# Attention keys in tiles of 128 with a shared slot for the rest, all scores inside FFN1 in groups of three, and centering in three steps

## The chip, the cores and the metric

The kernel runs on one core of one Trainium2 chip. The metric is the device time of one execution in microseconds (us), as the median of several executions.

The engines are called PE (TensorE, matmul), DVE (VectorE), ACT (ScalarE), POOL (GpSimd) and SP (SyncE, which here issues DMAs only).

## The reference, cut to what matters

```python
q, k, v: (8, 12, 448, 64)               # batch, heads, sequence, head size
scores = q @ k.T / sqrt(64)
attn   = max(scores, 0)**2 / 448        # no softmax: score tiles are independent
x      = attn @ v                       # -> (8, 448, 768)
xn     = (x - mean) / sqrt(var + 1e-6) * g_ln
out    = x + max(xn @ w_ch1, 0) @ w_ch2 # FFN, 768 -> 3072 -> 768
```

448 tokens are 3.5 tiles of 128.

## The kernel before: the parts that matter

Batch after batch, PE does FFN1 (24 groups of twelve matmuls), then FFN2. FFN2 works on pairs of 128-token tiles by a seven-product scheme of Strassen's kind. A batch has one or two such pairs (one in batches 0 and 4, where batch 0 uses the plain product); half tiles are carried over. The attention of batch b+1 is woven into batch b, in "excursions": a few score tiles between FFN matmuls. A "pair" of heads is two heads of 64 rows; a batch has six pairs.

```python
def att_T(i):                    # queries and keys of pair i, from batch 2 on: DMA transposes
    for t in range(2):
        nc.sync.dma_start_transpose(qkT[i][:, t, :]..., qk_ring[:, i % 3, t])
...
def att_QK(i, t, ...):           # one score slot: 112 keys x 448 queries, both heads
    for hh in range(2):
        nc.tensor.matmul(half[:SP, :S], qkT[i][r, 1, t*SP:(t+1)*SP], qkT[i][r, 0, :], ...)
...
def ffn_x(b, ki):                # the tokens of batch b back to token-major (x_tok has 5 slots)
    m0 = ts[0]
    while m0 < ts[-1] + 1:
        m1 = min(ts[-1] + 1, m0 + NT - m0 % NT)      # NT = 5: a batch that wraps needs two
        nc.sync.dma_start_transpose(x_tok[:, m0 % NT:...], xT[:, ki, ...])
        m0 = m1
...
def excursion(n, ...):
    while loads: load_qk(loads.pop(0))               # POOL issues loads
    if ready: att_AV(ready.pop(0), ...)              # weighted sum of values of a finished pair
    took = [slots.pop(0) for _ in range(n)]
    for m, (i, t) in enumerate(took): att_QK(i, t, ...)
    ...                                              # squares on DVE
    for i, t in took:
        if t == NJ - 1:
            ready.append(i); queued(i)               # queued(i): att_T(i + 3), later load_qk(i + 6)
...
def ffn_1_all(b):
    for ni in range(K2):                             # 24 groups
        if 3 <= ni < 3 + K1: ffn_x(b, ni - 3)        # x_tok transposes, six feature blocks
        ffn_1(ni)
        if m >= 0 and ni % 2 == 0: ffn_stats(ms[m])  # row statistics on DVE, late in FFN1
        if 0 < b < B - 1 and ni in IN_FFN1[b]: excursion(3, relus=(2,))
```

Both kinds of DMA transpose are issued by SP, in program order. Those of pair i+3 are put into the program when the last scores of pair i are; there are three qkT buffers.

## Time and profile before

| | before |
|---|---|
| time, median of 3 (lowest to highest); with a fourth execution 542.81 us | 542.84 us (541.98 to 544.71) |
| PE busy, granted clock | 97% of the span, 1.00 |
| FFN1 / FFN2 of a batch with two tile pairs (2, 3, 6) | 36.08 / 30.89 us |
| FFN1 / FFN2 of batch 4 (one pair) | 39.11 / 16.17 us |
| FFN1 of batch 7, which has no scores | 27.24 us |

A stage's length is the time from its first FFN matmul to the first one of the next stage, read from the timeline of matmuls. These are from the page of the kernel before: busy us of an engine with its share of the span, and the granted PE clock in 40 slices, in tenths.

```profile
PE 527.1 (97%) x5729; PEld 341.6 (63%) x5729; DVE 369.6 (68%) x660; ACT 306.6 (57%) x487; POOL 204.3 (38%) x261
...
PEclk9999999999999999999999999999999999999999
```

PE is the bottleneck, so what counts is which matmuls start late. The next lines are PE's timeline in FFN1 of batch 5: start and length in us, engine, source line, what is written from what, how many, and in brackets the idle time before and what ended it. L225 is the score matmul, L322 FFN1.

```profile
368.64 0.59 PE L225 MATMUL sc<-qkT_t 64*112 64x448 bf16 x4
...
369.35 3.60 PE L322 MATMUL f<-xc,w 128*64 128x448 bf16 x36
372.87 0.40 PE L225 MATMUL sc<-qkT_t 64*112 64x448 bf16 x2
374.14 0.40 PE L225 MATMUL sc<-qkT_t 64*112 64x448 bf16 x2 [0.87 <-DMA qkT_t<-qk_ring]
```

From the first line to the FFN1 line is an excursion without a wait: three slots in 0.71 us (368.64 to 369.35), against 3 x 0.189 us of streaming. The last line is a wait for a transpose of queries and keys. Its bracket gives PE's idle time, 0.87 us; from start to start it is 1.08 us (374.14 less 372.87, less the usual 0.19 us of one slot). Below, waits are told from start to start, so they are up to 0.2 us longer than the brackets. The SP queue in the same stretch shows why it came late (L300 issues x_tok transposes, L202 those of queries and keys):

```profile
350.41 7.61 SPq L300 DMA_TRANSPOSE x_tok<-xT  x6
358.19 2.50 SPq L202 DMA_TRANSPOSE qkT_t<-qk_ring  x2
360.73 8.63 SPq L300 DMA_TRANSPOSE x_tok<-xT  x6
369.53 6.51 SPq L202 DMA_TRANSPOSE qkT_t<-qk_ring  x5
```

Two transposes take 2.50 us, six take 7.61: about 1.25 us each, and SP does nothing else meanwhile. For 19 us it only works through transposes; batch 5 needs twelve for x_tok, because its four tiles wrap around the five slots.

The other thing that holds PE is centering in FFN2. This is DVE's timeline in FFN2 of batch 5 (L288 centers, L432 takes a product out of PSUM):

```profile
398.10 3.64 DVE L288 SCALAR_TENSOR_TENSOR xc<-f,g_sb,xc 128x448 bf16<-128x448 f32 x6 [2.67 <-PE f L282]
401.66 0.55 DVE L432 TENSOR_TENSOR acc<-f,acc 128x384 f32<-128x384 f32 x1
```

And this is PE's timeline behind it (L384 is a matmul of a product):

```profile
402.26 1.98 PE L384 MATMUL f<-w,h 128*64 128x384 bf16 x22 [0.36 <-DVE acc L432]
```

Six centering steps run in a row, and PE then waits for the evacuation behind them. From start to start the product is 0.53 us late.

### The profile page before, as it was taken

The numbers are of one execution on the slowest core, as the hardware profiler recorded it, in microseconds if no ns is written. First come the engines' busy times: TensorE is split into PE (matmuls) and PEld (weight loads), VectorE is DVE, ScalarE is ACT, GpSimd is POOL, SyncE is SP. The second block draws the span as 40 slices with busy tenths as digits, with TensorE's granted clock in tenths as the row PEclk, the third lists the DMA queues.
The fourth block names the chain that finished last, engine by engine and source line by source line (L and its number), as shares of the span: only waits on it lengthen the run. The fifth ranks groups of instructions, "written<-read, shape, count | busy, mean of one in ns | idle before, by whom it ended". The sixth has DMA issues, their size and how long they took to land. (4 is left out here: it accounts for less than half of the span.)

```text
span 541.1 us, 13784 instructions
## 1 busy us (share of the span) xinstructions
PE 527.1 (97%) x5729; PEld 341.6 (63%) x5729; DVE 369.6 (68%) x660; ACT 306.6 (57%) x487; POOL 204.3 (38%) x261
## 2 busy tenths in 40 slices
PE   8999999999999999999999999999999999999995
PEld 4445566556775567755677547655677556787785
DVE  4965678998746877468764779568774687730564
ACT  6957762667436674466734665466643667434321
POOL 8421138246452634525444236423635000330022
PEclk9999999999999999999999999999999999999999
DMA  9999999999239972499834879279923810132022
GB/s 160 195 191 207 204 174 162 106 102 112 56 90 120 90 65 59 94 122 93 70 69 85 82 92 119 63 86 97 106 56 86 96 20 3 31 91 50 8 61 60
DMA packets 163023, 51.88 MB, mean 96 GB/s; under 512 B 128784, under 2 KB 162960, under 8 KB 162960
## 3 DMA queue, kind: packets, MB, share of 16 engines
q0 software_dynamic: 94208, 25.74, 49.9%
q1 hardware_dynamic: 68256, 24.86, 24.7%
q8 instruction: 45, 0.74, 0.6%
q10 hardware_dynamic: 496, 0.40, 0.3%
q14 instruction: 18, 0.15, 0.1%
HBM read 51.91 MB, written 11.01 MB: 116 GB/s over the span
## 5 line engine op out<-in xcount | busy, mean ns | idle before, releaser
L322 PE MATMUL f<-xc,w 128*64 128x448 bf16 x2268 | 226.3, 353 | 0.4 <-ACT h L577 0.3
L322 PEld LDWEIGHTS <-w 128*64 128x64 bf16 x2268 | 130.6, 110 | 88.0 <-issue 16.9
L324 ACT ACTIVATE h<-f 128x448 bf16<-128x448 f32 x189 | 103.1, 546 | 99.3 <-PE f L322 98.8
L231 ACT ACTIVATE at<-sc 112x896 bf16<-112x896 f32 x149 | 128.4, 916 | 15.3 <-PE sc L225 15.0
L384 PE MATMUL f<-w,s_sb 128*64 128x384 bf16 (+2 forms) x1584 | 132.6, 324 | 1.2 <-DVE s_sb L378 1.2
L384 PEld LDWEIGHTS <-s_sb 128*64 128x64 bf16 x1584 | 103.9, 110 | 25.6 <-issue 2.7
L236 DVE TENSOR_TENSOR at<-at 112x896 bf16<-112x896 bf16 x177 | 100.8, 618 | 7.8 <-ACT at L231 7.7
L136 POOL DMA_DIRECT2D qk_ring<-in_q_dram x72 | 50.8, 711 | 105.3 <-DMA qkT_t<-qk_ring 85.6
L418 POOL TENSOR_TENSOR o_t<-o_t,x_tok 128x384 f32<-128x384 f32 x26 | 23.8, 914 | 139.1 <-ACT o_t L417 83.9
L229 DVE TENSOR_SCALAR at<-f 112x448 bf16<-112x448 f32 x86 | 49.5, 618 | 30.9 <-PE f L225 30.8
L378 DVE TENSOR_TENSOR s_sb<-h 128x1536 bf16<-128x1536 bf16 x65 | 63.3, 991 | 0.0
L136 POOL DMA_DIRECT2D qk_ring<-in_k_dram x72 | 50.3, 703 | 17.4 <-DMA w<-in_moe_w_ch_dram 11.4
L384 PE MATMUL f<-w,h 128*64 128x384 bf16 x624 | 54.3, 326 | 2.2 <-DVE acc L432 1.8
L418 POOL TENSOR_TENSOR acc<-acc,x_tok 128x384 f32<-128x384 f32 x25 | 35.9, 1442 | 42.4 <-ACT acc L417 42.4
L384 PEld LDWEIGHTS <-h 128*64 128x64 bf16 x624 | 41.0, 110 | 13.5 <-issue 3.7
L225 PE MATMUL sc<-qkT_t 64*112 64x448 bf16 x298 | 46.8, 375 | 1.6 <-DMA qkT_t<-qk_ring 1.3
L417 ACT ACTIVATE o_t<-f,rstd 128x384 f32<-128x384 f32 x26 | 14.9, 574 | 54.7 <-DVE acc L422 38.0
L260 DVE TENSOR_SCALAR xT<-f 128x448 bf16<-128x448 f32 x37 | 22.8, 616 | 30.2 <-PE f L250 20.9
L225 PEld LDWEIGHTS <-qkT_t 64*112 64x112 bf16 x384 | 20.0, 125 | 33.9 <-issue 26.4
L250 PE MATMUL f<-at,v_ring 112*64 112x448 bf16 x336 | 41.1, 354 | 0.1
L288 DVE SCALAR_TENSOR_TENSOR xc<-f,g_sb,xc 128x448 bf16<-128x448 f32 x48 | 29.1, 677 | 15.1 <-PE f L282 15.0
L417 ACT ACTIVATE acc<-acc,rstd 128x384 f32<-128x384 f32 x25 | 14.8, 610 | 34.8 <-DVE acc L432 33.4
(65 smaller groups left out, 341.5 us busy)
## 6 DMA issues: line engine op xcount, KB each, us to landing
w<-in_moe_w_ch_dram POOLq DMA_DIRECT2D x6, 768.0 KB, 27.6
w<-in_moe_w_ch_dram POOLq DMA_DIRECT2D x4, 1152.0 KB, 36.3
qk_ring<-in_q_dram POOLq DMA_DIRECT2D x72, 56.0 KB, 3.6
qk_ring<-in_k_dram POOLq DMA_DIRECT2D x72, 56.0 KB, 3.8
v_ring<-in_v_dram POOLq DMA_DIRECT2D x36, 112.0 KB, 4.0
out_dram<-o_t SPq DMA_DIRECT2D x9, 168.0 KB, 3.0
out_dram<-o_t SPq DMA_DIRECT2D x9, 144.0 KB, 2.1
x_tok<-xT SPq DMA_TRANSPOSE x72, 3.6
```

The source lines that it names most:

```text
L136: nc.gpsimd.dma_start(sb[:, :, x, :], src[b, 2 * a + x].rearrange("(p j) d -> p j d", j=NJ))
L225: nc.tensor.matmul(half[:SP, :S], qkT[i][r, 1, t * SP:(t + 1) * SP], qkT[i][r, 0, :], start=True, stop=True)
L229: nc.vector.tensor_scalar(at[:, hh], spare[hh][:SP, :S], 0.0, None, op0=Alu.max)
L231: nc.scalar.activation(at, ps[:SP, :, :S], Act.Relu)
L236: nc.vector.tensor_mul(attn[i, t], attn[i, t], attn[i, t])
L250: nc.tensor.matmul(ps[hh * D:(hh + 1) * D, :], v_of(i)[:, hh, t * D:(t + 1) * D], attn[i, t][:, hh, :], start=(t == 0), stop=(t == NJ - 1))
L322: nc.tensor.matmul(ps[c * D:(c + 1) * D, :], w1[:, ki, n0:n0 + D], xc[:, ki, :], start=(ki == 0), stop=(ki == K1 - 1))
L324: nc.scalar.activation(h[:, ni, CARRY:], ps, Act.Relu)
L378: nc.vector.tensor_tensor(s_sb[:, n], x, y, op=op)
L384: nc.tensor.matmul(ps[c * D:(c + 1) * D, :d1 - d0], stat[:, ki, c * D:(c + 1) * D], w2[:, slot, ki, d0:d1], start=(start and ki == 0), sto ...
L417: nc.scalar.activation(o_t, y, Act.Identity, scale=rstd[:, m:m + 1])
L418: nc.gpsimd.tensor_tensor(o_t, o_t, x_half(m, dh), op=Alu.add)
```

## The change

Its intent: fewer score slots (two pairs in 7 slots, not 8, because keys come in three full tiles of 128, and the last 64 keys of two heads of two pairs share one slot as four 64x64 matmuls), fewer excursions (seven of three slots, all in FFN1), and an FFN2 of products alone, with centering spread over three steps. The core of the diff, with cuts:

```diff
-    s_sb = big_pool.tile([P, 4, KH, P], bf16)
+    s_sb = big_pool.tile([P, 3, KH, P], bf16)
-    qk_ring = big_pool.tile([SP, 3, 2, 2 * NJ * D], bf16)
+    qk_ring = big_pool.tile([P, 3, 2, 2 * NJ * D], bf16)
...  load_qk: two loads of queries, two of full keys, one of last keys (4 -> 5)
...  load_v: one of full values, two of last values, other rows zero (1 -> 3)
     def att_T(i, copy=None):
-            for t in range(2):
-                nc.sync.dma_start_transpose(qkT[i][:, t, :]..., qk_ring[:, i % 3, t])
+            nc.sync.dma_start_transpose(qkT[i][:, 0, :]..., ring[:SP, 0])
+            nc.sync.dma_start_transpose(qkT[i][:, 1, :SF]..., ring[:, 1, :SF])
+            nc.sync.dma_start_transpose(qkT[i][:, 1, SF:], ring[:SS, 1, SF:])
     def att_QK(i, t, relu_by=None):
+        if keys == P and t == NF:                       # the shared slot
+            for x in range(2):
+                for hh in range(2):
+                    r0 = row0(i + x, hh)                # 64 * ((i + x + hh) % 2)
+                    nc.tensor.matmul(half[x][r0:r0 + SS], qkT[i + x][r, 1, SF:],
+                                     qkT[i + x][r, 0, :], start=True, stop=True)
     def center(b):
-        for ki in range(K1):
-            center_part(ki, mean_ps)
+        return [first, lambda: parts(2, 4), lambda: parts(4, 6)]
+    for i in range(PE_T * NPAIR, NP_ALL, 2):
+        slots += [(i, t) for t in range(NF + 1)] + [(i + 1, t) for t in range(NF)]
...
+    IN_FIRST = {3: 2, 6: 3, 9: 3, 12: 3, 15: 3, 18: 3, 20: 3, 22: 2}   # batch 0
+    IN_REST = (1, 4, 7, 10, 13, 16, 19)
+                if ni in IN_REST:
+                    excursion(3, relus=(2,), evac_by=nc.scalar if b == 1 else None)
+                if ni == IN_REST[-1] + 3:
+                    flush_loads()
+                    next_AV()                           # the sixth pair's output, on DVE
     def ffn_2_all(b):
-        ... excursions, weighted sums and gains between products ...
+            todo = [lambda k=k: (gain(b + 1, k), gain(b + 1, k + 1)) for k in range(0, K1, 2)]
+            todo += center(b + 1)
```

The diff also shortens the tail of the last tile pair.

More of the change, by code (lines that the diff above doesn't have):

```diff
@@ L37 @@
     SP = S // NJ
+    NF = S // P
+    SF = NF * P
+    SS = S - SF
     NPAIR = H // 2
@@ L47 @@
     c2 = (1.0 / D) / S
-    assert SP * NJ == S and NTILE * P == B * S and CARRY == S % (2 * P)
+    assert SP * NJ == S and SS == D and NTILE * P == B * S and CARRY == S % (2 * P)
     out_tok = out.rearrange("b (p j) d -> b p j d", j=NJ)
@@ L82 @@
     xs = big_pool.tile([P, S], bf16)
-    qk_ring = big_pool.tile([SP, 3, 2, 2 * NJ * D], bf16)
-    v_ring = big_pool.tile([SP, NPAIR, 2, NJ * D], bf16)
+    qk_ring = big_pool.tile([P, 3, 2, 2 * NJ * D], bf16)
+    v_ring = big_pool.tile([P, NPAIR, 2 * NJ * D], bf16)
     sc = []
@@ L119 @@
     v1_sb = s_sb.rearrange("p a k d -> p (a k d)")[:SP, :EARLY].rearrange("p (h e) -> p h e", h=H)
-    v0_sb = v_ring.rearrange("p a x e -> p (a x) e")
+    v0_sb = v_ring[:SP].rearrange("p a (x e) -> p (a x) e", x=2)
     first_qkv = {0: (early[:, 0], early[:, 1], v0_sb), 1: (early[:, 2], early[:, 3], v1_sb)}
@@ L129, in load_heads, with row0, v_full, v_last @@
                 src[b, h0:h0 + hs].rearrange("h (p j) d -> p h (j d)", j=NJ))
+    def row0(i, hh):
+        return D * ((i + hh) % 2)
     def load_qk(i):
         b, a = divmod(i, NPAIR)
-        for t, src in enumerate((q, k)):
-            sb = qk_ring[:, i % 3, t].rearrange("p (j x d) -> p j x d", x=2, j=NJ)
-            for x in range(2):
-                nc.gpsimd.dma_start(sb[:, :, x, :],
-                                    src[b, 2 * a + x].rearrange("(p j) d -> p j d", j=NJ))
+        ring = qk_ring[:, i % 3]
+        q_to = ring[:SP, 0].rearrange("p (j x d) -> p j x d", x=2, j=NJ)
+        k_to = ring[:, 1].rearrange("p (t x d) -> p t x d", x=2, t=NF + 1)
+        for x in range(2):
+            nc.gpsimd.dma_start(q_to[:, :, x, :],
+                                q[b, 2 * a + x].rearrange("(p j) d -> p j d", j=NJ))
+        for x in range(2):
+            nc.gpsimd.dma_start(k_to[:, :NF, x, :],
+                                k[b, 2 * a + x, :SF].rearrange("(p t) d -> p t d", t=NF))
+        nc.gpsimd.dma_start(k_to[:SS, NF], k[b, 2 * a:2 * a + 2, SF:].rearrange("x s d -> s x d"))
+    def v_full(a):
+        return v_ring[:, a, :2 * NF * D].rearrange("p (x e) -> p x e", x=2)
+    def v_last(a):
+        return v_ring[:, a, 2 * NF * D:].rearrange("p (x d) -> p x d", x=2)
     def load_v(i):
         b, a = divmod(i, NPAIR)
-        nc.gpsimd.dma_start(v_ring[:, a],
-                            v[b, 2 * a:2 * a + 2].rearrange("h (p j) d -> p h (j d)", j=NJ))
+        nc.gpsimd.dma_start(v_full(a),
+                            v[b, 2 * a:2 * a + 2, :SF].rearrange("h (p t) d -> p h (t d)", t=NF))
+        for x in range(2):
+            r0 = row0(i, x)
+            nc.gpsimd.dma_start(v_last(a)[r0:r0 + SS, x], v[b, 2 * a + x, SF:])
     def v_of(i):
         b, a = divmod(i, NPAIR)
-        return first_qkv[1][2][:, 2 * a:2 * a + 2] if b == 1 else v_ring[:, a]
+        return first_qkv[b][2][:, 2 * a:2 * a + 2]
     def load_early():
@@ L200, in att_T @@
             new_qkT(i)
-            for t in range(2):
-                nc.sync.dma_start_transpose(
-                    qkT[i][:, t, :].rearrange("p (j s) -> p j s", j=NJ), qk_ring[:, i % 3, t])
+            ring = qk_ring[:, i % 3]
+            nc.sync.dma_start_transpose(
+                qkT[i][:, 0, :].rearrange("p (j s) -> p j s", j=NJ), ring[:SP, 0])
+            nc.sync.dma_start_transpose(
+                qkT[i][:, 1, :SF].rearrange("p (t s) -> p t s", t=NF), ring[:, 1, :SF])
+            nc.sync.dma_start_transpose(qkT[i][:, 1, SF:], ring[:SS, 1, SF:])
             return
@@ L216, in att_T, with att_QK @@
         (copy or nc.vector.tensor_copy)(qkT[i], ps)
-    def att_QK(i, t, square=True, relu_by=None):
-        at = attn_pool.tile([SP, 2, S], bf16, tag="attn")
+    def att_QK(i, t, relu_by=None):
+        full = attn_pool.tile([P, 2, S], bf16, tag="attn")
+        keys = SP if i < PE_T * NPAIR else P
+        at = full[:keys]
         attn[i, t] = at
         ps = next_sc() if relu_by is not nc.vector else None
-        for hh in range(2):
-            r = slice(hh * D, (hh + 1) * D)
-            half = spare[hh] if ps is None else ps[:, hh]
-            nc.tensor.matmul(half[:SP, :S], qkT[i][r, 1, t * SP:(t + 1) * SP], qkT[i][r, 0, :],
-                             start=True, stop=True)
+        half = [bank[:keys, :S] for bank in (spare if ps is None else (ps[:, 0], ps[:, 1]))]
+        if keys == P and t == NF:
+            for x in range(2):
+                for hh in range(2):
+                    r = slice(hh * D, (hh + 1) * D)
+                    r0 = row0(i + x, hh)
+                    nc.tensor.matmul(half[x][r0:r0 + SS], qkT[i + x][r, 1, SF:], qkT[i + x][r, 0, :],
+                                     start=True, stop=True)
+        else:
+            for hh in range(2):
+                r = slice(hh * D, (hh + 1) * D)
+                nc.tensor.matmul(half[hh], qkT[i][r, 1, t * keys:(t + 1) * keys], qkT[i][r, 0, :],
+                                 start=True, stop=True)
         if ps is None:
-            for hh in range(2):
-                nc.vector.tensor_scalar(at[:, hh], spare[hh][:SP, :S], 0.0, None, op0=Alu.max)
-        else:
-            nc.scalar.activation(at, ps[:SP, :, :S], Act.Relu)
-        if square:
-            att_square(i, t)
+            for x in range(2):
+                nc.vector.tensor_scalar(at[:, x], half[x], 0.0, None, op0=Alu.max)
+        else:
+            nc.scalar.activation(at, ps[:keys, :, :S], Act.Relu)
     def att_square(i, t):
@@ L249, in att_AV @@
             for hh in range(2):
-                nc.tensor.matmul(
-                    ps[hh * D:(hh + 1) * D, :],
-                    v_of(i)[:, hh, t * D:(t + 1) * D],
-                    attn[i, t][:, hh, :],
-                    start=(t == 0), stop=(t == NJ - 1))
+                if b < PE_T:
+                    weights, values = v_of(i)[:, hh, t * D:(t + 1) * D], attn[i, t][:, hh, :]
+                elif t < NF:
+                    weights, values = v_full(pr)[:, hh, t * D:(t + 1) * D], attn[i, t][:, hh, :]
+                else:
+                    weights, values = v_last(pr)[:, hh], attn[i - i % 2, NF][:, i % 2, :]
+                nc.tensor.matmul(ps[hh * D:(hh + 1) * D, :], weights, values,
+                                 start=(t == 0), stop=(t == NJ - 1))
         if half == 0:
@@ L279, in center, with parts, first @@
         mean_ps = spare[1][:, :S]
-        for n, part in enumerate((xs, xT_of(b, K1 - 1))):
-            for c in range(2):
-                nc.tensor.matmul(mean_ps[c * D:(c + 1) * D, :], ones[:, :D], part,
-                                 start=(n == 0), stop=(n == 1))
-        for ki in range(K1):
-            center_part(ki, mean_ps)
+        def parts(k0, k1):
+            for ki in range(k0, k1):
+                center_part(ki, mean_ps)
+        def first():
+            for n, part in enumerate((xs, xT_of(b, K1 - 1))):
+                for c in range(2):
+                    nc.tensor.matmul(mean_ps[c * D:(c + 1) * D, :], ones[:, :D], part,
+                                     start=(n == 0), stop=(n == 1))
+            parts(0, 2)
+        return [first, lambda: parts(2, 4), lambda: parts(4, 6)]
     def center_part(ki, mean_ps):
@@ L372, in plain_part @@
             store(o_t, m, dh * HD, (dh + 1) * HD)
-    s_turn = Turns(range(4))
+    s_turn = Turns(range(3))
     def sum_of(x, y, op):
@@ L423, in after5 @@
             finish(new_o(), c, m1, 1)
+            before7()
         def after2():
@@ L429, in after2, with before7 @@
             finish(new_o(), d, m2, 0)
+        def before7():
+            if last:
+                scaled_plus(acc1, acc1, m1, x_half(m1, 0))
         def after7():
+            if last:
+                scaled_plus(acc1, a, m1, acc1)
+                store(acc1, m1, 0, HD)
+                return
             tt(acc1, a, acc1, op=Alu.add)
@@ L481, with flush_loads @@
     loads = []
+    def flush_loads():
+        while loads:
+            load_qk(loads.pop(0))
     def queued(i):
@@ L487, in queued, with ends, next_AV, excursion @@
                 loads.append(i + 6)
-    def step_a(i):
-        att_QK(i, 0, square=False)
-        att_QK(i, 1, square=False)
-        if i == NPAIR + 1:
-            att_T(i + 1)
-        for t in range(2):
-            att_square(i, t)
-    def step_b(i):
-        att_QK(i, 2, square=False)
-        att_QK(i, 3, square=False)
-        if i > NPAIR:
-            att_AV(i - 1)
-            if i + 2 < PE_T * NPAIR:
-                att_T(i + 2)
-        else:
-            att_T(i + 1)
-        for t in range(2, NJ):
-            att_square(i, t)
-        queued(i)
-    slots = [(i, t) for i in range(PE_T * NPAIR, NP_ALL) for t in range(NJ)]
-    ready = []
-    def excursion(n, bank=None, evac_by=None, relus=(), square_by=nc.vector):
-        while loads:
-            load_qk(loads.pop(0))
+    slots = [(NPAIR, t) for t in range(2, NJ)]
+    slots += [(i, t) for i in range(NPAIR + 1, PE_T * NPAIR) for t in range(NJ)]
+    for i in range(PE_T * NPAIR, NP_ALL, 2):
+        slots += [(i, t) for t in range(NF + 1)] + [(i + 1, t) for t in range(NF)]
+    ready = []
+    def ends(i, t):
+        if i < PE_T * NPAIR:
+            return [i] if t == NJ - 1 else []
+        if i % 2 == 0:
+            return [i] if t == NF else []
+        return [i] if t == NF - 1 else []
+    def next_AV(**how):
         if ready:
-            att_AV(ready.pop(0), bank=bank, evac_by=evac_by)
+            att_AV(ready.pop(0), **how)
+    def excursion(n, relus=(), evac_by=None):
+        flush_loads()
+        next_AV(evac_by=evac_by)
         took = [slots.pop(0) for _ in range(n)]
         for m, (i, t) in enumerate(took):
-            att_QK(i, t, square=False, relu_by=nc.vector if m in relus else nc.scalar)
+            att_QK(i, t, relu_by=nc.vector if m in relus else nc.scalar)
         for i, t in took:
-            if square_by is nc.scalar:
-                nc.scalar.activation(attn[i, t], attn[i, t], Act.Square)
-            else:
-                att_square(i, t)
+            att_square(i, t)
         for i, t in took:
-            if t == NJ - 1:
-                ready.append(i)
-                queued(i)
+            for e in ends(i, t):
+                ready.append(e)
+                queued(e)
     def step_fine(i):
-        att_QK(i, 0, square=False)
+        att_QK(i, 0)
         if 0 < i < NPAIR - 1:
@@ L538, in step_fine @@
         att_QK(i, 1)
+        att_square(i, 1)
         if i == 0:
@@ L543, in step_fine @@
             att_AV(i - 1, 0)
-        att_QK(i, 2, square=False)
+        att_QK(i, 2)
         if i == 0:
@@ L550, in step_fine @@
         att_QK(i, 3)
+        att_square(i, 3)
         if i > 1:
@@ L563, in first_end @@
         att_AV(i - 1, 1)
-        att_QK(i, 0, square=False)
-        att_QK(i, 1, square=False)
+        att_QK(i, 0)
+        att_QK(i, 1)
         mean_part(i - 1)
@@ L579, in ffn_1_first @@
             att_square(NPAIR, t)
-    def second_steps():
-        yield lambda: step_b(NPAIR)
-        for i in range(NPAIR + 1, PE_T * NPAIR):
-            yield lambda: step_a(i)
-            yield lambda: step_b(i)
+    IN_FIRST = {3: 2, 6: 3, 9: 3, 12: 3, 15: 3, 18: 3, 20: 3, 22: 2}
+    T_IN_FIRST = {4: 1, 7: 2, 10: 3, 13: 4, 16: 5}
+    IN_REST = (1, 4, 7, 10, 13, 16, 19)
     def ffn_1_all(b):
-        steps = second_steps() if b == 0 else None
         ms = tiles_of(b)
@@ L601, in ffn_1_all @@
                 w2_sums(*LATE_SUMS[SUMS_AT.index(ni)])
-            if b == 0 and ni % 2 == 1:
-                next(steps)()
-            if 0 < b < B - 1 and ni in IN_FFN1[b]:
-                excursion(3, relus=(2,))
-        assert steps is None or next(steps, None) is None
+            if b == 0:
+                if ni in IN_FIRST:
+                    excursion(IN_FIRST[ni], relus=(2,))
+                if ni in T_IN_FIRST:
+                    att_T(NPAIR + T_IN_FIRST[ni])
+            elif b < B - 1:
+                if ni in IN_REST:
+                    excursion(3, relus=(2,), evac_by=nc.scalar if b == 1 else None)
+                if ni == IN_REST[-1] + 3:
+                    flush_loads()
+                    next_AV()
     SUMS_AT = (0, 3, 6, 9, 12, 15)
@@ L611 @@
                                      (B21, B21, B11, Alu.subtract)) for part in range(2)]
-    ONE = [b for b in range(B) if ((b + 1) * S // (2 * P)) - (b * S // (2 * P)) == 1]
-    IN_FFN1 = {b: (1, 4, 7, 10, 13, 16, 19, 22) if b in ONE else (2, 5, 8, 11, 14, 17, 20)
-               for b in range(B)}
     def ffn_2_first():
@@ L625, in ffn_2_first @@
                     if n == 1:
-                        att_AV(PE_T * NPAIR - 1, bank=spare[0])
+                        next_AV(bank=spare[0])
+                        assert not ready
                     if n < K1 - 1:
@@ L632, in ffn_2_first @@
                         gain(1, K1 - 2)
-                        center(1)
+                        for step in center(1):
+                            step()
                     if n == 8:
@@ L644, in ffn_2_all @@
         x_bank, y_bank = f_turn.items
-        z_bank, av_bank = spare
+        z_bank = spare[0]
         first = b * S // (2 * P)
@@ L648, in ffn_2_all @@
         banks = [x_bank, z_bank, y_bank] if len(pairs) == 2 else [z_bank, x_bank, y_bank]
-        gains = list(range(K1)) if b < B - 1 else []
-        centered = [b == B - 1]
+        todo = []
+        if b < B - 1:
+            assert not ready
+            todo = [lambda k=k: (gain(b + 1, k), gain(b + 1, k + 1)) for k in range(0, K1, 2)]
+            todo += center(b + 1)
         def between(n):
@@ L655, in between @@
                 carry(b)
-            if b == B - 1:
-                return
-            if slots_left():
-                if n in (1, 3):
-                    excursion(min(2, slots_left()), av_bank, nc.scalar, square_by=nc.scalar)
-            elif ready:
-                att_AV(ready.pop(0), bank=av_bank, evac_by=nc.scalar)
-            done = (b + 2) * NPAIR - len(ready) - NPAIR * (b + 1)
-            done -= sum(1 for i, t in slots if t == NJ - 1 and i < (b + 2) * NPAIR)
-            if not gains and not centered[0]:
-                center(b + 1)
-                centered[0] = True
-            for _ in range(2):
-                if gains and gains[0] < done:
-                    gain(b + 1, gains.pop(0))
-        def slots_left():
-            return sum(1 for i, t in slots if i < (b + 2) * NPAIR)
+            if todo:
+                todo.pop(0)()
         for pr in pairs:
@@ L678, in ffn_2_all @@
             banks = banks[1:] + banks[:1]
-        assert centered[0] and not gains
+        assert not todo
     E = mybir.EngineType
@@ L704 @@
         load_w2(B22, 1, 1)
+        nc.gpsimd.memset(v_ring[:, :, 2 * NF * D:], 0.0)
         for i in range(PE_T * NPAIR, (PE_T + 1) * NPAIR):
```

## The prediction

> **What bounds it now.** TensorE is busy 97% of the span (page, part 1). In the timeline of matmuls a batch with two tile pairs takes 66.97 us: FFN1 36.08, FFN2 30.89. Pure streaming in it: FFN1 27.24 us, fourteen products 27.5, centering 0.38, six attention outputs 4.5, 24 score slots 4.5. From start to start, an excursion (scores between FFN matmuls) costs about 0.26 us beyond streaming: 97+44 ns going in, 94+24 ns coming out. [...] In FFN2, "acc" on VectorE after six centering steps (3.64 us in a row) holds TensorE for 0.37 us (chain of waits, timeline).
>
> **What the change saves.**
> - Scores of batches 2 to 7: 126 slots, not 144: 18 x 0.189 = 3.4 us, if the four 64x64 matmuls of a shared slot run together.
> - Excursions after batch 0 fall from 53 to 42, score groups in batch 0 from 11 to 8: 14 x 0.26 = 3.6 us.
> - A shared slot is a third tiling shape: up to 24 more switches, estimate 0.12 us each: up to -3 us.
> - Centering stalls go: about 3 us. Stalls of 0.65, 0.87 and 1.08 us on qkT would go too.
> - ScalarE squares (15 x 0.96 us) go, off the critical path. FFN2 becomes plain products, as in the last batch (27.5 us).
>
> Summed by stage (FFN1 about 38, FFN2 27.7, batch 4's 14.05), without new waits: about 532 us.
>
> **What it adds: transposes on one queue.** The SP queue issues every DMA transpose in order, 1.2 to 1.25 us each whatever its size, landing 2.4 to 3.6 us after issue. A pair now needs three (queries, keys, last keys), not two, all in FFN1, among the x_tok transposes. Those are twelve, not six, in batches 1, 4 and 5, where the tiles wrap around the five x_tok slots; just there the trace already has its qkT stalls. Scores also run ahead: the fifth pair's transposes (counted within a batch) were needed 27.5 us into FFN1, now at 22.5. My queue estimate: start at 4.4 us (after the stores), ten x_tok transposes and three of the fourth pair, so the fifth pair's keys are issued at about 23 and land at about 26: a stall near 4 us in the fifth excursion. The sixth pair's last-key transpose comes 7.75 us later, TensorE needs it after 5: another 2.7 in the sixth. About 6.5 us in each of the three batches, 20 in all, on the critical path: no matmul overtakes another in this trace. Batches 2, 3, 6 have 2 to 4 us of slack.
>
> GpSimd has eight loads a pair, not five, 0.7 us each: nearly full in FFN1.
>
> **Sum.** 532 + 20 = 552 if the queue estimate holds in full; it may be too harsh: 547 us, range 531 to 556. Faster by over 2%: 0.12; within 2%: 0.63; slower by over 2%: 0.25.
>
> **What would show it.** Right: matmul waits of 2 to 5 us on qkT transposes in batches 1, 4 and 5 alone, twice each; two-pair batches 2, 3, 6 at about 65.8 us; FFN2 at 27.7; shared slots near 0.19 us plus a switch; no centering stall. Wrong: shared slots at 0.38 us; no qkT waits (then about 532); waits also in batches 2, 3, 6; a granted clock below 1.0 after the longer stalls.

## The result, and the profile after

561.16 us, median of 4 (559.03 to 562.49), against 542.81 us for the kernel before: a ratio of 1.0329, 95% interval 1.0287 to 1.0371. That is slower by 3.3%, and above the range predicted. (A ratio here is the mean time of one kernel's runs over that of the other's of the same rounds, so it is not quite the ratio of the medians.)

| stage, us (profiled run) | before | after | sum predicted without new waits |
|---|---|---|---|
| FFN1 of batches 1, 4, 5 | 37.18, 39.11, 37.13 | 47.30, 44.93, 48.53 | 38 |
| FFN1 of batches 2, 3, 6 | 36.08, 36.08, 36.08 | 39.29, 39.06, 38.60 | 38 |
| FFN2, two tile pairs | 30.88 to 30.91 | 27.67 to 27.68 | 27.7 |
| FFN2 of batch 4 | 16.17 | 14.03 | 14.05 |
| FFN1 of batch 0, from the fourth group | 36.62 | 37.35 | 35.8 (36.62 less 3 x 0.26; not in the prediction) |

FFN2 came out as summed, and it gives 18 us in all. FFN1 took that back and 18 us more. The page after:

```profile
PE 530.8 (95%) x5729; PEld 352.9 (63%) x5729; DVE 381.1 (68%) x674; ACT 274.4 (49%) x442; POOL 266.3 (48%) x369
...
PEclk9999999979999999999999989998899999999999
```

PE's busy share fell and its granted clock dips three times: in batches 1, 4 and 5. PE's timeline in batch 5 (L261 is a score slot, L256 a shared slot, L367 FFN1, L290 a weighted sum of values):

```profile
379.21 0.55 PE L261 MATMUL sc<-qkT_t 64*128 64x448 bf16 x4
383.46 0.55 PE L261 MATMUL f<-qkT_t 64*128 64x448 bf16 x2 [3.70 <-DMA qkT_t<-qk_ring]
383.95 4.83 PE L367 MATMUL f<-xc,w 128*64 128x448 bf16 x36
...
389.95 0.38 PE L256 MATMUL f<-qkT_t 64*64 64x448 bf16 x2
392.82 0.38 PE L256 MATMUL f<-qkT_t 64*64 64x448 bf16 x2 [2.49 <-DMA qkT_t<-qk_ring]
```

The wait sits in the third slot of the fifth excursion, and another in the shared slot of the sixth. The FFN1 block between them takes 4.83 us where the same block took 3.60 before: the clock. SP's queue in that stretch (L345 is x_tok; L224, L226, L228 are queries, full keys, last keys):

```profile
362.37 5.05 SPq L345 DMA_TRANSPOSE x_tok<-xT  x4
367.58 1.20 SPq L224 DMA_TRANSPOSE qkT_t<-qk_ring  x1
368.88 1.19 SPq L226 DMA_TRANSPOSE qkT_t<-qk_ring  x1
370.17 1.17 SPq L228 DMA_TRANSPOSE qkT_t<-qk_ring  x1
371.39 8.25 SPq L345 DMA_TRANSPOSE x_tok<-xT  x6
379.81 1.20 SPq L224 DMA_TRANSPOSE qkT_t<-qk_ring  x1
381.12 1.19 SPq L226 DMA_TRANSPOSE qkT_t<-qk_ring  x1
```

PE wanted the fifth pair at about 379.6 us; SP began to issue its transposes at 379.81, directly after six for x_tok, and the keys landed shortly before 383.46. Even the transpose of only 64 last keys takes 1.17 us to issue.

The clock is best seen in windows of batch 1: the wait of 5.2 us, the 36 matmuls behind it, and a stretch 1.7 us later (window; busy us and instructions of each engine; then the granted clock, third from the end):

```profile
112.80:117.90 5.10, 0.16 (x2) 0.00 (x0) 0.39 (x1) 1.90 (x3) 0.59 (x1) 0.90 0.39 65
118.50:124.40 5.90, 5.90 (x38) 3.00 (x38) 5.17 (x9) 1.09 (x2) 4.15 (x7) 0.56 1.16 118
126.10:129.50 3.40, 3.40 (x40) 2.07 (x38) 3.40 (x8) 2.48 (x4) 2.88 (x5) 1.00 1.24 121
```

After the wait the clock was 0.56, and PE is busy all the time (5.90 of 5.90 us): busy share did not show this loss. In batch 1 the granted clock was 0.5 for 6.83 us (from 116.84 us on), and for 3.41 us at each of three other waits (from 325.06, 383.08 and 393.32 us on); matmul starts were 366 to 373 ns apart instead of 189 (342 to 365 in the last step of each). Over the whole run I counted 39 such slow steps, about 7.1 us.

A third new wait sits where FFN1 ends. This is DVE's timeline at the end of FFN1 of batch 2 (L359 and L360 are row statistics, L297 evacuates the sixth pair's output):

```profile
202.63 0.54 DVE L359 BATCH_NORM_STATS2 stats<-x_tok 128x6 f32<-128x384 bf16 x1
203.21 0.21 DVE L360 BATCH_NORM_AGGREGATE mv_sb<-stats 128x2 f32<-128x12 f32 x1
203.34 0.58 DVE L297 TENSOR_SCALAR xT<-f 128x448 bf16<-128x448 f32 x1
```

And PE's timeline there (L429 is the first product of FFN2):

```profile
203.97 0.84 PE L429 MATMUL f<-w,h 128*64 128x384 bf16 x8 [0.49 <-DVE xT L297]
```

The statistics of the last tiles stand in DVE's queue ahead of the evacuation of the bank that FFN2 needs first. Start to start this costs 0.55 to 0.75 us in six stages, 3.9 us.

Last, the shared slot itself, in an excursion of batch 2 where it is the middle one:

```profile
181.31 0.36 PE L261 MATMUL sc<-qkT_t 64*128 64x448 bf16 x2
181.60 0.38 PE L256 MATMUL sc<-qkT_t 64*64 64x448 bf16 x4
181.92 0.36 PE L261 MATMUL f<-qkT_t 64*128 64x448 bf16 x2
182.21 1.14 PE L367 MATMUL f<-xc,w 128*64 128x448 bf16 x10
```

Its four matmuls start within 11 ns of each other (so in 13 of the 18 shared slots; in the other five the second pair's keys came late), so they do run together, as hoped. But this excursion takes 0.90 us, against 0.67 us for three plain slots; with the shared slot first or last it takes 0.80. One middle and two outer ones a batch cost 0.48 us, 2.9 us over six batches, most of the 3.4 us that 18 fewer slots give. So much did a third shape cost here; what PE does in that time was not shown.

### The profile page after: what moved, and what is told of

Its sections match the earlier page's. It is cut to its first block, busy times and chain, and to the rows that moved or that the text cites. A ratio compares the mean times of both kernels' runs of the same rounds, so it can differ in the third digit from the quotient of the medians.

```text
span 559.2 us, 14134 instructions
## 1 busy us (share of the span) xinstructions
PE 530.8 (95%) x5729; PEld 352.9 (63%) x5729; DVE 381.1 (68%) x674; ACT 274.4 (49%) x442; POOL 266.3 (48%) x369
## 4 chain that ended last, share of the span: by engine, by line
PE 74%; DVE 9%; DMA 8%; SPq 4%; POOL 2%; issue 2%; ACT 0%; POOLq 0%; DVEq 0%; ACTq 0%
PE f L429 32%; PE f L367 28%; DMA qkT_t<-qk_ring 5%; PE f L290 4%; PE sc L261 3%; PE f L412 3%; SPq L345 2%; DVE full L270 2%; DVE full L265 2%; DMA qk_ring<-in_k_dram 2%; DVE xT L297 2%; DMA w<-in_k_dram 1%; DVE stats L359 1%; PE f L261 1%; DVE stats L358 1%
## 5 line engine op out<-in xcount | busy, mean ns | idle before, releaser
L367 PE MATMUL f<-xc,w 128*64 128x448 bf16 x2268 | 235.1, 361 | 0.7 <-ACT h L369 0.4
L367 PEld LDWEIGHTS <-w 128*64 128x64 bf16 x2268 | 134.2, 112 | 92.2 <-issue 25.9
L429 PE MATMUL f<-w,s_sb 128*64 128x384 bf16 (+2 forms) x1584 | 130.5, 324 | 0.0
L429 PEld LDWEIGHTS <-s_sb 128*64 128x64 bf16 x1584 | 110.1, 110 | 17.2
L267 ACT ACTIVATE full<-sc 128x896 bf16<-128x896 f32 (+1 forms) x126 | 108.2, 916 | 16.0 <-PE sc L261 15.8
L270 DVE TENSOR_TENSOR full<-full 128x896 bf16<-128x896 bf16 (+1 forms) x174 | 98.5, 617 | 5.9 <-ACT full L267 5.7
L265 DVE TENSOR_SCALAR full<-f 128x448 bf16<-128x448 f32 (+1 forms) x96 | 55.4, 617 | 37.8 <-PE f L261 35.5
L297 DVE TENSOR_SCALAR xT<-f 128x448 bf16<-128x448 f32 x43 | 26.5, 616 | 42.8 <-PE f L290 33.3
L429 PE MATMUL f<-w,h 128*64 128x384 bf16 x624 | 53.2, 326 | 2.3 <-DVE xT L297 2.3
L429 PEld LDWEIGHTS <-h 128*64 128x64 bf16 x624 | 43.6, 110 | 10.7 <-issue 3.7
L164 POOL DMA_DIRECT2D v_ring<-in_v_dram x72 | 39.9, 573 | 11.2 <-DMA w<-in_moe_w_ch_dram 10.3
L290 PE MATMUL f<-full,v_ring 128*64 128x448 bf16 (+1 forms) x336 | 40.5, 354 | 0.1
L463 POOL TENSOR_TENSOR acc<-acc,x_tok 128x384 f32<-128x384 f32 x24 | 28.1, 1176 | 22.6 <-ACT acc L462 22.6
L261 PEld LDWEIGHTS <-qkT_t 64*128 64x128 bf16 (+1 forms) x312 | 13.1, 103 | 40.4 <-issue 21.9
L261 PE MATMUL sc<-qkT_t 64*128 64x448 bf16 (+1 forms) x228 | 35.5, 365 | 0.3 <-DVE qkT_t L241 0.2
```

Of the source, the lines that this page charges most:

```text
L261: nc.tensor.matmul(half[hh], qkT[i][r, 1, t * keys:(t + 1) * keys], qkT[i][r, 0, :], start=True, stop=True)
L265: nc.vector.tensor_scalar(at[:, x], half[x], 0.0, None, op0=Alu.max)
L267: nc.scalar.activation(at, ps[:keys, :, :S], Act.Relu)
L270: nc.vector.tensor_mul(attn[i, t], attn[i, t], attn[i, t])
L290: nc.tensor.matmul(ps[hh * D:(hh + 1) * D, :], weights, values, start=(t == 0), stop=(t == NJ - 1))
L367: nc.tensor.matmul(ps[c * D:(c + 1) * D, :], w1[:, ki, n0:n0 + D], xc[:, ki, :], start=(ki == 0), stop=(ki == K1 - 1))
```

## The experiments

Theory A: SP issues one transpose in 1.2 us whatever its size (medians in the change: 1.18 us for last keys, 1.20 for queries and for full keys, 1.23 for x_tok); twelve x_tok transposes and three per pair, all in FFN1, make those of the fifth and sixth pair late in batches 1, 4 and 5. Rival B: the loads through POOL are late (eight a pair, not five). Rival C: the halved clock is a cost of its own, on top of the queue. Rival D: the transposes land late because of the traffic beside them. All runs have four timed executions. All outputs are right.

| run | median us | ratio to before | granted clock (profiled) |
|---|---|---|---|
| after | 561.16 | 1.0329 | 0.983 |
| a_one_piece | 545.96 | 1.0053 | 0.994 |
| b_one_piece | 540.46 | 0.9963 | 1.000 |
| a_split_all | 580.07 | 1.0698 | 0.971 |
| a_fill | 564.44 | 1.0420 | 0.986 |
| a_two_T | 552.03 | 1.0174 | 0.992 |
| a_one_two | 538.82 | 0.9929 | 0.998 |
| a_one_two_av | 534.51 | 0.9854 | 0.998 |
| b_all_ffn1 | 547.63 | 1.0093 | 0.999 |
| best | 531.29 | 0.9789 | 0.999 |
| best_center_one | 540.13 | 0.9943 | 0.999 |
| b_center_three | 539.71 | 0.9937 | 0.997 |
| b_all_center_three | 541.35 | 0.9977 | 0.997 |

The kernel before had medians of 542.35 to 543.11 us in these rounds.

### a_one_piece: six x_tok transposes instead of twelve

A half tile carried over occupies one of the five slots. With another choice of first slot, each batch still lies in one piece, and no memory is added.

```diff
+    FIRST_SLOT = (2, 0, 0, 0, 2, 0, 0, 0)
+    def slot(m):
+        b = max(b for b in range(B) if b * S // P <= m)
+        return FIRST_SLOT[b] + m - b * S // P
-        while m0 < ts[-1] + 1: ...            # up to two pieces
+        nc.sync.dma_start_transpose(x_tok[:, slot(m0):slot(m0) + n, ...], xT[:, ki, c0:c0 + n * P])
```

> The changed kernel, with other x_tok slots: each batch's tiles lie side by side in the same five slots, so each feature block needs one x_tok transpose in batches 1, 4 and 5 too (6 a batch, not 12). Theory A (the qkT transposes wait behind x_tok transposes on the SP queue): waits on qkT of batches 1, 4, 5 fall from 5.2, 4.2+0.9, 3.9+2.7 us to under 1 us, the granted clock is 1.00, FFN1 of batches 1, 4, 5 falls from 47.3, 44.9, 48.5 to about 39 us, time about 538 us (534 to 541). Rival B (the loads through GpSimd, eight a pair, or their landing, make the transposes late): waits stay, time over 553 us.

Measured: 545.96 us, 15 us faster than the change. FFN1 of batches 1, 4, 5 fell to 42.83, 38.83, 42.61 us. So A holds and B falls as the main cause, since no load was touched. But 538 was expected, and waits of 0.7 to 2.2 us stayed in the sixth excursion of batches 2 to 5 (and 1.0 and 1.6 us in the fourth and fifth of batch 1). PE's timeline in batch 2 of this run (L256 is the shared slot):

```profile
187.58 0.38 PE L256 MATMUL f<-qkT_t 64*64 64x448 bf16 x2
189.09 0.38 PE L256 MATMUL f<-qkT_t 64*64 64x448 bf16 x2 [1.13 <-DMA qkT_t<-qk_ring]
```

The last-key transpose of that pair was issued at 183.87 us and let PE go on at 189.09, 5.2 us later. I had reckoned with 2.4 to 3.6 us. (The median landing of the three qkT transposes is 3.6 to 3.9 us in this run, against 3.2 to 3.4 in the change, so landings grew when the queue was relieved; why was not tested.) So 2 to 4 us of slack in batches 2, 3 and 6 was too kind.

### b_one_piece: the same slots in the kernel before

The same edit. 

> The kernel before with the same slots. A: its three waits on qkT (0.65, 0.87, 1.08 us in batches 1, 4, 5) go, time about 540.2 us against 542.8. B: no change.

Measured: 540.46 us, just as expected. All three waits on qkT are gone; in batch 1 an FFN1 group now waits 0.55 us for an attention output on DVE instead.

### a_split_all: more transposes, same bytes

```diff
             m1 = min(ts[-1] + 1, m0 + NT - m0 % NT)
+            if b in (2, 3, 6) and m0 == ts[0]:
+                m1 = m0 + 2
```

> The changed kernel with the x_tok transposes of batches 2, 3 and 6 cut in two as well (12 there, same bytes). A: these three batches now wait like batches 1, 4, 5, FFN1 47 instead of 39 us, granted clock below 0.98, time about 583 us (575 to 590). B: within 2 us of 561.

Measured: 580.07 us. FFN1 of batches 2, 3, 6 went from 39.29, 39.06, 38.60 to 45.61, 45.55, 47.81 us, with waits of 3.4, 4.0 and 5.5 us in the fifth excursion. The bytes were the same and the time grew by 18.9 us: what counted here is the number of transposes. This and a_one_piece move the same term up and down by about the same amount.

### a_fill: PE kept busy during the wait

```diff
             for m, (i, t) in enumerate(took):
+                if m == 2 and t == 0 and i in FILL:       # fifth pair, made in batches 1, 4, 5
+                    for _ in range(26):
+                        nc.tensor.matmul(spare[1][:, :256], ones, w1[:, 0, :256], start=True, stop=True)
```

> The changed kernel with 26 matmuls of 256 columns (2.8 us, result unused) before the score slot that waits in the fifth excursion of batches 1, 4 and 5[...]. Rival C (the halved clock after the long waits adds its own 7 us on top of the queue's delay): clock 1.00 and about 554 us. Theory A (the queue sets when TensorE can go on; slow matmuls mostly fill time until the sixth pair's keys land): clock near 1.00, but the wait in the sixth excursion grows to 2 or 3 us in batches 1 and 4, and time falls by 3 us at most (558 or more).

Measured: 564.44 us, 3 us slower, not faster. PE's timeline in batch 1 of this run (L574 is the filling):

```profile
114.23 3.01 PE L574 MATMUL f<-w,ones 128*128 128x256 bf16 x26
119.14 0.36 PE L261 MATMUL f<-qkT_t 64*128 64x448 bf16 x2 [1.90 <-DMA qkT_t<-qk_ring]
119.44 3.60 PE L367 MATMUL f<-xc,w 128*64 128x448 bf16 x36
...
127.02 0.38 PE L256 MATMUL f<-qkT_t 64*64 64x448 bf16 x2 [2.44 <-DMA qkT_t<-qk_ring]
```

The 36 matmuls run at full speed again (3.60 us). But PE then reached the sixth pair sooner and waited there: 2.6, 2.7 and 3.5 us in batches 1, 4, 5, against 0, 0.9 and 2.7 in the change. The clock fell there in turn, as I read the trace (granted clock 0.986 over the run, 0.983 in the change). From the end of the fifth wait to the end of the sixth it was 7.9, 8.0 and 8.7 us here, at full clock, and 7.8 us or more in batches 4 and 5 of the change (7.80, 9.36), at half clock; in batch 1 of the change the sixth pair's last keys landed 7.7 us after the fifth wait ended. So rival C falls for the 30 slow steps between the two excursions: they filled time until the queue delivered. It was not tested for the nine steps (1.6 us) after the sixth wait of batch 5. My expectation of a small gain was wrong as well. The profiled execution was the slowest of the four (569.0 us), and half of its loss is from batch 3, whose sixth excursion waited 2.9 us in this run (0.25 in the change). Why that wait varies so much stays open.

### a_two_T: keys with one transpose

```diff
-        qkT_t = t_pool.tile([P, 2, S], bf16, tag="qkT")
+        qkT_t = t_pool.tile([P, S + (NF + 1) * P], bf16, tag="qkT")   # keys: 512 columns
-            nc.sync.dma_start_transpose(qkT[i][:, 1, :SF]..., ring[:, 1, :SF])
-            nc.sync.dma_start_transpose(qkT[i][:, 1, SF:], ring[:SS, 1, SF:])
+            nc.sync.dma_start_transpose(kT[i].rearrange("p (t s) -> p t s", t=NF + 1), ring[:, 1])
+        nc.gpsimd.memset(qk_ring[SS:, :, 1, 2 * NF * D:], 0.0)
```

> The changed kernel with the keys of a pair transposed by one instruction (the 64 last keys and 64 rows of zeros with the full ones, into a 512-column key part): two qkT transposes a pair, as before, not three; x_tok transposes still 12 in batches 1, 4, 5. Theory A: one transpose (1.3 us) less ahead of the fifth pair's keys, three less ahead of the sixth's: waits in the fifth excursion of batches 1, 4, 5 near 3.9, 2.9, 2.6 us, those in the sixth excursion gone in every batch, time about 545 us (541 to 549). Rival B (loads): the loads are the same, so no change, over 556 us.

Measured: 552.03 us, 9 us faster than the change, where 16 was expected. The waits in the fifth excursion fell to 4.3, 2.7 and 3.3 us, near the expected 3.9, 2.9 and 2.6; in batches 2 and 3 none is left (FFN1 38.6 us). In the sixth excursion 0.6, 1.5 and 0.5 us stay. The direction is A's, the size was over-reckoned.

### a_one_two and a_one_two_av: both together, then the end of FFN1

a_one_two is a_one_piece and a_two_T together. a_one_two_av adds:

```diff
-                    next_AV()
+                    next_AV(evac_by=nc.scalar)
-                    excursion(IN_FIRST[ni], relus=(2,))
+                    excursion(IN_FIRST[ni], relus=(2,), evac_by=nc.scalar if ni == 22 else None)
```

> Both relieved: one x_tok transpose a feature block and two qkT transposes a pair. Theory A: no wait on qkT over 0.5 us anywhere, clock 1.00, FFN1 of batches 1 to 6 at 38 to 39 us, time about 537 us (535 to 540). What is left over 532 us would be the wait for the attention output before FFN2 (0.55 to 0.75 us in seven stages, 4 us). Rival D (the landing of a transpose is slowed by the loads that now run beside it, whatever the queue): waits of 1 us and more stay, 541 or more.

> As a_one_two, with the last attention output of each FFN1 (and of batch 0) evacuated by ScalarE, not VectorE, which has the row statistics of the last tiles queued ahead of it. If that queue is the cause, the waits of 0.55 to 0.75 us at the start of FFN2 go, and the time falls by 3 to 4 us to about 533 us (531 to 536).

Measured: 538.82 and 534.51 us. FFN1 of batches 2, 3, 5, 6 is 38.6 us with the first and 37.89 with the second, where pure counting had given 38. No transpose wait is left in batches 2 to 6, so D falls as what holds PE there: the traffic is still there. (Landings are slower than in the change, a median of 3.8 to 3.9 us for the qkT transposes; they only come early enough now.) The evacuation is worth the 4.3 us between the two runs. Batch 1 alone still waits 2.8 us in its fifth excursion.

### best: batch 1 and the first loads

SP's queue of a_one_two_av at the start of batch 1 shows a different reason there:

```profile
94.48 2.74 SPq L350 DMA_TRANSPOSE x_tok<-xT  x2
98.97 1.25 SPq L226 DMA_TRANSPOSE qkT_t<-qk_ring  x1
102.04 1.20 SPq L228 DMA_TRANSPOSE qkT_t<-qk_ring  x1
```

SP stands idle between 97.2 and 98.97, and from 100.2 to 102.04: it waits for the loads of queries and keys (the last of each landed at 98.84 and 101.91), which POOL issues behind all value loads of batch 2. So rival B is right here, in one batch.

```diff
+            for n in LATE_V.get(i, ()):      # values of pairs 14 to 17 (from zero) after keys 15 to 17
+                load_v(n)
-            load_v(i)
+            if i < PE_T * NPAIR + 2:
+                load_v(i)
```

> As a_one_two_av, with the first loads reordered: the keys and queries of the sixteenth to eighteenth pair are issued before the values of pairs 15 to 18 (counting all pairs from one), which are needed 10 to 35 us later. In batch 1 the transposes still waited for qk_ring loads behind eighteen loads of values on GpSimd. If so, the last wait on qkT (2.8 us, batch 1) goes: FFN1 of batch 1 falls from 41.3 to about 38.5 us, time about 531.7 us (530 to 533). If batch 1 waits for the queue and not for the loads: no change, 534.5.

Measured: 531.29 us (530.78 to 532.53), ratio 0.9789, interval 0.9771 to 0.9807: faster than the kernel before, though whether by 2% is unclear. FFN1 of batch 1 fell from 41.30 to 39.04 us, where 38.5 was expected, and its wait on qkT is gone. SP's queue at the start of batch 1 in best:

```profile
96.66 2.67 SPq L350 DMA_TRANSPOSE x_tok<-xT  x2
99.49 1.23 SPq L226 DMA_TRANSPOSE qkT_t<-qk_ring  x1
100.89 1.19 SPq L228 DMA_TRANSPOSE qkT_t<-qk_ring  x1
```

The first of these transposes still starts 0.2 us late, no longer 1.8, and the second follows at once. This version beats both kernels, and it is the change itself with its queues served: 5.3% faster than the change by the medians, and close to the 532 us that the prediction had summed for a change without new waits.

### Centering: best_center_one, b_center_three, b_all_ffn1, b_all_center_three

best_center_one is best with the six centering steps in one; b_center_three is the kernel before with three steps; b_all_ffn1 is the kernel before with all 24 slots in eight excursions in FFN1; b_all_center_three is both.

```diff
best_center_one:
-        return [first, lambda: parts(2, 4), lambda: parts(4, 6)]
+        return [lambda: (first(), parts(2, 4), parts(4, 6))]
b_center_three:
-                center(b + 1)
+                todo.extend(center(b + 1))           # three steps of two
+            if todo:
+                todo.pop(0)()
b_all_ffn1:
-    IN_FFN1 = {b: (1, 4, ..., 19, 22) if b in ONE else (2, 5, ..., 17, 20)
+    IN_FFN1 = {b: (1, 4, 7, 10, 13, 16, 19, 22)
```

> As best, with centering in one step of six as in the kernel before. If the six in a row hold up the sums and evacuations of the products, FFN2 grows from 27.7 to 28.2 us or, as in b_all_ffn1 (1.33 us a stage), to 29: 3 to 8 us slower than best, about 535 to 540 us. If the three steps do nothing: the same as best.

> The kernel before with centering in three steps and nothing else. The six stalls behind it (0.53 us each, 1.33 in batch 4) go: about 539.3 us (538 to 541). If they are no part of the chain: 542.4.

> The kernel before with only the schedule changed: all 24 score slots of a batch (keys in four tiles of 112) inside FFN1 in eight excursions of three, none in FFN2; centering and transposes as they were. By the cost of an excursion (0.26 us) five batches save one each, 1.3 us; the qkT waits of batches 1, 4, 5 stay near 1 us or go: 540 to 542.5 us. If the early scores alone were what the queue cannot serve: over 547 us.

> b_all_ffn1 with centering in three steps: the 1.33 us stalls of six stages go, so about 540 us (538.5 to 542) against 547.6; then all scores inside FFN1 with four tiles of 112 keys is worth about what its fewer excursions are.

Measured: 540.13, 539.71, 547.63 and 541.35 us. Three steps are worth 3.4 us in the old schedule (FFN2 30.3 instead of 30.9, and 14.8 instead of 16.2 in batch 4) and 8.8 us in the new one, where FFN2 grows from 27.7 to 29.06 us without them. PE's timeline in best_center_one, batch 2 (L432 is a product, waiting for a sum that DVE forms behind the six steps):

```profile
208.56 2.14 PE L432 MATMUL f<-w,s_sb 128*64 128x384 bf16 x24 [1.17 <-DVE s_sb L426]
```

b_all_ffn1 was expected at 540 to 542.5 and came out at 547.6, because emptying FFN2 of scores brings centering forward to where DVE also has sums to form: the wait went from 0.53 to 1.33 us. With three steps this goes (541.35), though a transpose wait of 3.0 us appears in batch 5 there. So putting all scores into FFN1 was worth nothing by itself in either form. That it pays together with the 128-key tiles and three centering steps is read from best alone: no run has those tiles without all scores in FFN1.

## Why the prediction was wrong, point by point

- *"PE bound; 0.26 us per excursion; FFN2 becomes plain products; FFN1 about 38; about 532 us without new waits."* Right. FFN2 measured 27.68 and 14.03 us, predicted 27.7 and 14.05. FFN1 without waits is 37.89 us in best, and best takes 531.3 us.
- *"If the four 64x64 matmuls run together; up to -3 us for the third shape."* Right: within 11 ns of each other, and 2.9 us given back, read from the trace alone. Sharing a slot hardly pays on PE.
- *"Waits of 2 to 5 us on qkT in batches 1, 4 and 5 alone, twice each."* The mechanism was right, in the place named. Fifth excursion: 5.2, 4.2, 3.9 us (predicted near 4). Sixth: none, 0.9, 2.7 (predicted 2.7 each). Sum 16.9 us, predicted 20. The experiments confirm it: halving the x_tok transposes gives back 15 us, doubling them elsewhere costs 19.
- *"It may be too harsh: 547 us, range 531 to 556."* This is the step that failed: the sum of what the queue costs. It was put at 20 us in all, then cut to 15 by a discount behind which no number stood, with the fall of the clock at nothing. The runs showed 24.0 us: 16.9 us of waits and 7.1 us of slow matmuls. With the 3.9 us of the last attention output, which the sum left out, that is 27.9 us against the 20 of the full sum, 552. So 7.9 of the 9.2 us between 552 and 561.16 are found, and 1.3 us are not.
- *The granted clock.* It stood in the list of what would make the prediction wrong, and was costed at zero: 39 slow steps, 7.1 us. a_fill shows that most of it is no cost on top of the queue, since PE without slow matmuls waited longer at the next transpose: the 30 steps after the fifth excursions (5.4 us), with the 3.6 us of waits in the sixth, stand where the prediction had 2.7 us of waits in each batch, 8.1 in all. The queue, its waits and these slow stretches are one cost: taking the queue's load away gave 22.3 us (561.16 to 538.82), of which the predicted 20 was most.
- *What was left out.* The last attention output behind the row statistics on DVE: 3.9 us by the trace, 4.3 us by experiment.
- *"Batches 2, 3, 6 have 2 to 4 us of slack."* Too much. They waited 0.5 us at most in the change, but up to 1.7 us in a_one_piece, where a landing took 5.2 us and not 3.6. I had read landing times off three waits instead of the spread of all transposes: in the kernel before one took 7.2 us.
- *"GpSimd nearly full in FFN1."* It was no cause in batches 2 to 6. In batch 1 it was, through the order of the first loads (2.8 us once the queue was freed), which I had not looked at.
- *Not settled:* why the sixth excursion's wait varies from run to run (0.25 to 2.9 us in batch 3), and what the shorter tail gave.

## What to carry to other kernels

Count the issues of every in-order queue per stage, with their measured time each, and compare with the time at which the consumer needs the result; a busy share did not show this one. When a sum from the profile says 552, don't shade it toward a nicer number: what was missing from this sum was further cost, the slow clock after the long waits (7.1 us) and the last evacuation (3.9 us). And when a schedule is moved, test its parts together: centering in three steps was worth 3.4 us before and 8.8 us after.

## What the traces show of transposes, the clock and tiling

- Transposes issued by SP: in the change 154 of 180 took 1.17 to 1.25 us, from 64 rows by 128 columns to 128 by 512, and 16 took over 1.5, up to 2.2 us; landings had a median of 3.3 us after issue, but went up to 7.7 us.
- The granted clock: in the change PE had four waits of over 1.1 us of idle time after the start of the kernel (5.04, 4.08, 3.70 and 2.49 us), and each came with a fall to 0.5 and 7 to 14 slow steps. In a_split_all the 36 matmuls behind a wait of 3.26 us took 6.36 us. But behind 1.90 us in a_fill and 2.61 us in a_one_two_av they took the usual 3.60, and the 1.17 us of the kernel before, in batch 4, came with no fall. So among these the length of the wait alone does not tell: 2.49 us came with a fall, 2.61 us without. What brings the fall about was not shown.
- Matmuls on one PSUM bank: in the shared slot two matmuls of different row halves write partitions 0-63 and 64-127 of one bank; they started 2 to 4 ns apart in the change and the result was right. Two row tiles on the same partitions were not run.
- A change of tile shape: it was 0.26 us for going from 128x64 tiles to the 64x112 of the kernel before and back (97+44 and 94+24 ns, as predicted), 0.22 us with the 64x128 tiles of the change (95+8 and 91+21 ns), and 0.13 to 0.23 us more for a 64x64 slot beside them.
